# A spectral mixer: a smaller first constant table, its masks, two moved loads and a new order of the jobs

## The chip, the cores and the metric

The kernel runs on one core of one Trainium2 chip. Its time is the device time of one execution in microseconds (us); the number compared is the median of several runs. A core has five engines that work at the same time and meet only at semaphores: TensorE (PE: matmuls, with weight loads shown as PEld), VectorE (DVE), ScalarE (ACT), GpSimd (POOL) and SyncE (SP). SP, ACT and POOL also issue DMAs, each on a queue of its own, in the order of its instructions.

## The reference

Two spectral filters on one input `x` (2048 x 1024), mixed by a gate for each row. Both filters have the same input, so only their products with the weights differ:

```python
X = jnp.fft.rfft2(x.astype(jnp.float32), axes=(-2, -1))
X = X * (w_r + 1j * w_i)                          # weights 2048 x 513
y = jnp.fft.irfft2(X, s=(S, D), axes=(-2, -1)).astype(jnp.bfloat16)
...
g = jax.nn.sigmoid((x * gate_w).sum(-1, keepdims=True))
return g * a + (1 - g) * b                        # a, b: y for the weights A and B
```

## The kernel before, in words

The two-dimensional transforms are built from matmuls with small tables of cosines and sines, in stages:

- **Stage 1** (L463, L457): the first step of the transform over rows. `x` comes in eight chunks c (two loads each, `xload`, L362: one by SP, one by ACT for c < 4, both by SP after). `prep` (L426, job `pp`) lets DVE write a reversed copy of half of a chunk into a zone; chunk 6 is folded by an addition and a subtraction instead. Each chunk gives two jobs `s1.c.j` of eight matmuls: four read `x` itself, four the reversed copy. The right-hand side is the table M of cosines and sines, and M times +1, -1 by partition, made by the jobs `mv.c.k` (`mvariant`, L417, on DVE at L424 or on ACT at L422) with scales from the sign table SM. M holds a column for each of two halves of the partitions (b), zero where a partition belongs to the other half: 2048 columns. It is loaded in four pieces (`MP`, L355; `mload`, L358). ACT or DVE then copies a job's 1024 columns out of PSUM (`evict1`, L467, recorded at the copy helpers L329 and L332).
- **Stage 2** (L494, jobs `s2`) and **stage 4** (L509, `s4`) give the spectrum, in two sets of columns: M (upper) and O (lower), eight units each; ACT empties PSUM after each (`e2`, `e4`). Units 2q and 2q+1 of stage 4 make pair q. Pairs lie in three slots (`direct`, L351), and their exchanged twins in two (`swapped`).
- **Exchange** (`swap`, L519, jobs `sw`): two POOL DMAs swap the odd and even partitions of a pair.
- **Products** (`product`, L529, recorded at L539): DVE multiplies a pair (D) and its exchanged twin (S) by the weights, in two halves: `D.M.0.1` is set M, pair 0, half 1. The upper halves of M's products must be done before the weights of set O (`wo`, L843) may be loaded over M's.
- **Stage 5** (L601, jobs `s5`, 32 of them): the first step back; groups 16 to 31 need all M products, 0 to 15 all O products. ACT (and DVE twice) empties PSUM (`e5`). `edge` (L664) puts right a few special columns.
- **Gate**: `gate_weights`, `gate_spectrum` (L554) and `row_sums` (L573) get the gate's row sums from the spectrum; they go to DRAM (`gate_rows`), come back broadcast to all partitions (`rows_in`, L637, job `zl`, two loads ZB0 and ZB1), and go through a sigmoid on ACT (L645, `sg`), a sign on DVE (L649, `gm`) and 16 products with the table U5 on DVE (L657, `rb`).
- **Stages 6 and 7** (L708, L732): the steps to the output rows; ACT and DVE (L776) finish them, SP stores.

The order of the jobs is written out by hand in `PLAN` (L151): a list of tokens, name, arguments, for jobs on PE the PSUM unit (0 to 3, two banks each), and the engine (`a` ACT, `d` DVE). Each engine runs its jobs in that order; the class `Prog` (L200) turns reads and writes of named buffers into semaphore waits. Before the first job stand 11 matmuls on zeros (L379); `IDLE` (L442) puts a few more matmuls whose result is not used ahead of two jobs of stage 1.

The loads at the start stand in this order. SP: M0, x chunk 0 (second half), M1, x chunks 1, 2, 3 (first halves), M3, then x chunks 4 to 7 and the weights. ACT: x chunk 0 (first half), chunk 1 (second half), M2, chunks 2 and 3 (second halves). POOL: SM. `late_loads` (L617) brings U5 and another table behind the last exchange, on SP, after the gate broadcast.

Of the kernel before, what the change touches and what calls it, by code (L numbers as in the profile page):

```python
# [5 lines left out]
ACT = mybir.ActivationFunctionType  # L6
# [16 lines left out]
def make_consts():  # L23
# [4 lines left out]
    M = np.zeros((128, 32, 16, 2, 2))  # L28
    for b in range(2):
        on = 1.0 * (pb == b)[:, None]  # L30
        n = 64 * n1[:, None] + 32 * b + np.arange(32)[None, :]
        for t in range(16):
            if t == 0:
                M[:, :, 0, 0, b] = on
                M[:, :, 0, 1, b] = on * ((-1.0) ** n1)[:, None]
            else:
                ph = pi2 * t * n / 2048
                M[:, :, t, 0, b] = on * np.cos(ph)
                M[:, :, t, 1, b] = -on * np.sin(ph)
    C["M"] = M.reshape(128, 2048)  # L40
# [58 lines left out]
    blocks += [np.ones((128, 128))]  # L99
# [15 lines left out]
    SM = np.zeros((128, 5), np.float32)  # L115
# [4 lines left out]
    SM[:, 4] = -1.0  # L120
    C["SM"] = SM
# [30 lines left out]
mv.0.3..d mv.0.2..d mv.0.1..d pp.0..d s1.0.0.0.pe mv.1.3..d mv.1.2..a mv.1.1..d s1.0.1.1.pe e1.0.0..a e1.0.1..d  # L152
mv.3.3..a mv.2.2..a mv.3.2..a mv.2.3..d mv.2.1..a pp.1..d s1.1.0.2.pe mv.3.1..a s1.1.1.3.pe e1.1.0..a pp.2..d
s1.2.0.0.pe e1.1.1..a s1.2.1.1.pe pp.3..d e1.2.0..a s1.3.0.2.pe e1.2.1..a mv.4.2..d mv.5.2..d s1.3.1.3.pe
mv.4.1..d e1.3.0..a mv.4.3..d pp.4..d s1.4.1.0.pe mv.6.1..d e1.3.1..a mv.5.1..d mv.7.1..d s1.4.0.1.pe mv.7.3..d
pp.5..d e1.4.1..a mv.7.2..d mv.5.3..d e1.4.0..a s1.5.0.2.pe pp.6..d s1.5.1.3.pe e1.5.0..a s1.6.0.0.pe pp.7.0..d
e1.5.1..a pp.7.1..d s1.7.0.1.pe e1.6.0..d s1.6.1.2.pe e1.7.0.0..a s1.7.1.3.pe e1.7.0.1..d e1.6.1..a
s2a.M.0.0.pe e1.7.1.1..d e1.7.1.0..a s2a.M.1.1.pe s2b.M.0..pe s2.M.2.2.pe e2.M.0..a s2b.M.1..pe e2.M.2..a
s4.M.0.3.pe e2.M.1..d s2.M.3.0.pe e4.M.0..a s4.M.1.2.pe e2.M.3..a s4.M.2.1.pe e4.M.1..a s4.M.3.3.pe e4.M.2..a
D.M.0.1..d sw.M.0..dma gw.0.pe s2.M.5.2.pe e4.M.3..a D.M.0.0..d s2.M.4.1.pe egw..a sw.M.1..dma e2.M.5..a  # L160
gs.1.3.pe e2.M.4..a D.M.1.1..d s4.M.5.0.pe egs.1..a s4.M.4.2.pe D.M.1.0..d e4.M.5..a gs.3.1.pe e4.M.4..a
s2.M.7.3.pe S.M.0.1..d egs.3..a s2.O.1.0.pe e2.M.7..a S.M.0.0..d gs.2.2.pe e2.O.1..a S.M.1.1..d s4.M.7.1.pe
sw.M.2..dma egs.2..a s2.M.6.3.pe S.M.1.0..d e4.M.7..a gs.0.0.pe e2.M.6..a D.M.2.1..d s2.O.0.2.pe egs.0..a
# [103 lines left out]
def bass_gated_mix__spectral_gfnet__spectral_gfnet__prompt_kernel(nc, A_x, A_w_r, A_w_i, B_x, B_w_r, B_w_i, gate_w, out):  # L267
# [25 lines left out]
    VT = sb("VT", 512, f32)  # L293
    SM = sb("SM", 5, f32)
# [23 lines left out]
    ONo = ck(22)  # L318
# [36 lines left out]
    MP = ((0, 4), (4, 8), (8, 16), (16, 32))  # L355
    mpiece = lambda r: next(i for i, (a, b) in enumerate(MP) if a <= r < b)

    def mload(i, eng):  # L358
        a, b = MP[i]
        dma(eng, f"M{i}", sl(XR, 64 * a, [(1, 64 * (b - a))]).bitcast(u16), cst["M"].ap()[:, 64 * a:64 * b], w=[("M", i)])  # L360
# [21 lines left out]
    dma("pool", "SM", SM[:], cst_sm.ap(), w=["SM"])  # L382
# [34 lines left out]
    def mvariant(eng, c, k):  # L417
        o, i = sl(XR, 2048 * k + 256 * c, [(1, 256)]), sl(XR, 256 * c, [(1, 256)])
        kw = dict(r=[("M", mpiece(4 * c)), "SM"], w=[("MV", c, k)])
        sc = SM[:, {1: 2, 2: 4, 3: 3}[k]:][:, :1]  # L420
        if eng == "act":
            P.add("act", lambda e: e.activation(o, i, ACT.Copy, scale=sc), **kw)  # L422
        else:
            P.add("dve", lambda e: e.tensor_scalar(out=o, in0=i, scalar1=-1.0 if k == 2 else sc, scalar2=None, op0=ALU.mult), **kw)  # L424

    def prep(c, j=None):  # L426
# [7 lines left out]
        for h in (1, 0):  # L434
# [514 lines left out]
```

## Time and profile before

| | |
|---|---|
| Time, median of 3 runs | 121.89 us (121.63 to 122.32) |
| The profiled execution's own time | 122.8 us |
| Its span, from the first to the last recorded instruction | 121.0 us |
| TensorE clock granted, mean | 0.997 of full speed |
| DMA traffic | 26.87 MB, 222 GB/s on average |
| M table, four loads | 64, 64, 128 and 256 KB |
| CK table, its last load (CL) | 416 KB |

The page of the profile gives the busy time of each engine, the span in 40 slices, the chain of work that ended last (each step led back to what released it), and groups of equal instructions: engine, operation, output <- input, shape, count, then busy time and mean duration, then the idle time of the engine ahead of them with what ended it. The chain and the timelines have one piece in a line: start and duration in us, engine, buffer, source line, count. A name such as `L601` is line 601 of the kernel. Engine names with a q (SPq, ACTq) are the instruction queues that issue DMAs; the view of DMA issues has, last in a line, the time from issue to landing.

### The profile page before, as it was taken

To read this page: it belongs to the slowest core of one execution; us is meant where nothing else is said; L and a number is where in the kernel's file an instruction comes from. 1 tells how busy PE (TensorE), PEld (TensorE's weight loads), DVE (VectorE), ACT (ScalarE), POOL (GpSimd) and SP (SyncE) were. 2 spreads that over 40 slices of the span, in tenths; PEclk is the share of its full clock that TensorE was granted. 3 is DMA by queue.
4 is the path that set the end of the run, shared out by engine and by line. 5 is a ranking of instruction groups with operands and counts; after the bars stand their busy time and mean duration, and the time that the engine had idled before them with its cause. 6 is when DMAs were issued, how large, how long until landed. Compare 5 with 4: busy or idle time off the path is not lost.

```text
span 121.0 us, 3622 instructions
## 1 busy us (share of the span) xinstructions
PE 113.5 (94%) x1546; PEld 99.1 (82%) x1546; DVE 85.8 (71%) x127; ACT 103.5 (86%) x127; POOL 17.3 (14%) x37
## 2 busy tenths in 40 slices
PE   6979999999999999789999989999899999999990
PEld 2358899969689787488799989999899989999980
DVE  0375667319679969999979917999503879787772
ACT  0498999699878999979999989999979688988861
POOL 4000009306003393030530000000000000000000
PEclk9999999999999999999999999999999999999998
DMA  2999999999999999649893999300000334443344
GB/s 61 296 331 370 348 360 332 321 319 344 371 350 325 353 306 256 185 108 277 152 371 117 297 381 418 122 0 5 0 0 5 126 134 173 176 175 119 146 175 173
DMA packets 27519, 26.87 MB, mean 222 GB/s; under 512 B 10208, under 2 KB 23216, under 8 KB 27248
## 3 DMA queue, kind: packets, MB, share of 16 engines
q1 hardware_dynamic: 24368, 20.85, 55.8%
q0 software_dynamic: 1760, 4.49, 10.2%
q10 hardware_dynamic: 1376, 1.31, 3.5%
q8 instruction: 12, 0.20, 0.7%
q14 instruction: 3, 0.02, 0.1%
HBM read 18.23 MB, written 4.20 MB: 185 GB/s over the span
## 4 chain that ended last, share of the span: by engine, by line
PE 42%; DVE 17%; DMA 16%; ACT 12%; issue 5%; SPq 4%; POOL 0%; DVEq 0%; ACTq 0%; POOLq 0%
PE PS L732 11%; PE PS L708 10%; PE PS L463 10%; DMA XR<-XR 10%; ACT WB L329 9%; DVE WA L539 9%; DVE WB L539 5%; PE PS L601 5%; SPq L326 4%; DMA WA<-in_B_w_i_dram 4%; PE PS L494 3%; DMA SM<-c_SM 3%; ACT XR L329 2%; ACT WA L329 2%; DVE WA L776 1%
## 5 line engine op out<-in xcount | busy, mean ns | idle before, releaser
L601 PE MATMUL PS<-CK,WA 128*128 128x128 bf16 x256 | 31.8, 223 | 1.6 <-DVE WA L539 1.6
L601 PEld LDWEIGHTS PS<-CK,WA 128*128 128x128 bf16 x256 | 31.3, 145 | 1.9 <-DVE WA L539 1.9
L329 ACT ACTIVATE XR<-PS 128x1024 bf16<-128x1024 f32 x31 | 29.5, 1035 | 2.9 <-PE PS L494 1.6
L329 ACT ACTIVATE WB<-PS 128x1024 bf16<-128x1024 f32 (+1 forms) x31 | 30.8, 1040 | 1.4 <-PE PS L601 1.2
L601 PE MATMUL PS<-CK,WB 128*128 128x128 bf16 x256 | 31.9, 226 | 0.0
L601 PEld LDWEIGHTS PS<-CK,WB 128*128 128x128 bf16 x256 | 31.3, 145 | 0.1
L329 ACT ACTIVATE WA<-PS 128x1024 bf16<-128x1024 f32 (+5 forms) x34 | 25.3, 807 | 5.5 <-PE PS L708 2.8
L776 DVE TENSOR_TENSOR WA<-PS,WA 128x512 bf16<-128x512 f32 (+1 forms) x30 | 19.7, 711 | 10.7 <-ACT WA L329 10.5
L539 DVE TENSOR_TENSOR WB<-XR,WA 128x2048 bf16<-128x2048 bf16 x16 | 19.1, 1222 | 3.3 <-ACT XR L329 2.6
L539 DVE TENSOR_TENSOR WA<-XR,WA 128x2048 bf16<-128x2048 bf16 x16 | 18.7, 1224 | 2.9 <-DMA XR<-XR 2.8
L732 PE MATMUL PS<-FT,WA 128*128 128x256 bf16 x140 | 17.6, 273 | 0.2 <-ACT WA L329 0.2
L494 PE MATMUL PS<-F,FT 128*128 128x128 bf16 x256 | 16.0, 219 | 0.0
L494 PEld LDWEIGHTS PS<-F,FT 128*128 128x128 bf16 x256 | 14.8, 98 | 0.9
L509 PE MATMUL PS<-XR,CK 128*128 128x512 bf16 (+1 forms) x72 | 15.3, 355 | 0.0
L732 PEld LDWEIGHTS PS<-FT,WA 128*128 128x128 bf16 x140 | 13.1, 98 | 1.6 <-ACT WA L329 0.4
L708 PE MATMUL PS<-XR,WB 128*128 128x128 bf16 x208 | 13.6, 219 | 0.5 <-ACT WB L329 0.4
L708 PEld LDWEIGHTS PS<-XR,WB 128*128 128x128 bf16 x208 | 12.5, 98 | 1.0 <-ACT WB L329 0.8
L329 ACT ACTIVATE FT<-PS 128x1024 bf16<-128x1024 f32 (+1 forms) x14 | 12.4, 988 | 0.3 <-PE PS L463 0.3
L326 POOL DMA_DIRECT2D XR<-XR x16 | 8.4, 529 | 25.1 <-DVE WA L539 12.5
L509 PEld LDWEIGHTS PS<-XR,CK 128*128 128x128 bf16 x72 | 6.5, 97 | 5.1 <-ACT XR L329 0.2
L463 PE MATMUL PS<-XR,WB 128*128 128x256 bf16 x56 | 8.4, 273 | 0.9 <-DMA WB<-in_A_x_dram 0.6
L463 PE MATMUL PS<-XR 128*128 128x256 bf16 x56 | 8.4, 273 | 0.2 <-DVE XR L332 0.2
(74 smaller groups left out, 88.1 us busy)
## 6 DMA issues: line engine op xcount, KB each, us to landing
XR<-XR POOLq DMA_DIRECT2D x16, 256.0 KB, 4.9
out_dram<-WA SPq DMA_DIRECT2D x15, 256.0 KB, 2.0
WB<-in_A_x_dram SPq DMA_DIRECT2D x12, 256.0 KB, 6.9
FT<-c_U SPq DMA_DIRECT2D x2, 1024.0 KB, 9.6
WA<-in_A_w_r_dram SPq DMA_DIRECT2D x7, 192.5 KB, 4.9
WA<-in_A_w_i_dram SPq DMA_DIRECT2D x7, 192.5 KB, 5.0
WA<-in_B_w_r_dram SPq DMA_DIRECT2D x7, 192.5 KB, 5.0
WA<-in_B_w_i_dram SPq DMA_DIRECT2D x7, 192.5 KB, 5.9
```

The source lines that it names most:

```text
L326: return P.add(eng, lambda e: e.dma_start(dst, src), dma=name, **kw)
L329: return P.add("act", lambda e: e.activation(dst, src, ACT.Copy), **kw)
L463: P.add("pe", lambda e, o=ps(u * 1024 + q * 256, [(1, 256)]), lh=lh, rh=rh, s=s, q=q: e.matmul(o, lh, rh, start=(s == 0 and q % 2 == 0), s ...
L494: P.add("pe", lambda e, o=o, lh=fblock(cmb, j, t), j=j, rh=rh, cmb=cmb: e.matmul(o, lh, rh, start=(j == 0 and cmb == 0), stop=(j == 1), sk ...
L509: P.add("pe", lambda e, o=o, fb=FB[kind, pm, m], m=m, rh=rh: e.matmul(o, sl(CK, fb, [(1, 128)]), rh, start=(m == 0), stop=(m == 1)), r=["C ...
L539: pop[st, q, sw, half] = P.add("dve", lambda e: e.tensor_tensor(out=o, in0=x, in1=w, op=ALU.mult), r=xr(o_, 2048) + wk, a=[("prod", st, sw ...
L601: P.add("pe", lambda e, o=o, lh=sl(t, to + l0, [(hp, 128)]), ab=ab: e.matmul(o, lh, KI(ab), start=(ab == 0), stop=(ab == 1)), r=[("prod", ...
L708: P.add("pe", lambda e, o=o, lh=lh, rh=rh, cp=cp: e.matmul(o, lh, rh, start=(cp == 0), stop=(cp == 1)), r=[("Z", pi), ("RB", r)], w=[("ps" ...
L732: P.add("pe", lambda e, lh=lh, rh=rh, st=st, sp=sp: e.matmul(ps(bank * 512 + o, [(1, 256)]), lh, rh, start=st, stop=sp), r=[("Y", r), "DI" ...
L776: P.add("dve", lambda e, s=s, op=op: e.tensor_tensor(out=sl(WA, outc(r) + 512 * s, [(1, n), (2, 256)]), in0=ps(2 * u * 512, [(256, n), (1, ...
```

## The change

1. **M without zeros.** The table is stored with one column for both halves of the partitions: 1024 columns in three pieces, rows 0 to 4, 4 to 16 and 16 to 32 (32, 96 and 128 KB). It is loaded to a place of its own; two new variants, k = 0 and 4, spread it: M times a mask that is 1 on the one half of the partitions and 0 on the other. SM gets the two masks as columns 5 and 6. The variants 1, 2 and 3 are made from those two, for a whole piece at a time (twice the piece's columns), and a stage 1 job waits for all that it uses before its first matmul.
2. **Order of columns.** The right-hand sides of stage 1 are now 32 columns from each of four places for each half of the transform's sign (eight pieces of 32 in 256, where four pieces of 64 stood); the PSUM output is written in pieces of 32 so that `evict1` reads the halves next to each other, and FT has another layout, from which stage 2 reads blocks of 128 as before.
3. **Loads.** SM is issued first on ACT's queue instead of POOL's. M2 is issued by ACT after chunk 2, not after chunk 1; there is no M3.
4. **Gate broadcast.** Both loads of `rows_in` also wait for the last exchange.
5. **Memory.** A block of ones at the end of CK goes (CL 416 to 384 KB); the tile VT of `row_sums` goes, and its data lie in the region that CL fills later.
6. **Job table.** `PLAN` is a new list: the same jobs of stages 2 to 7, in another order and on other PSUM units; `mv` jobs by piece; `e1.0.1` on ACT and `e1.2.0` on DVE, where it was the other way round; `e4.M.0` on DVE instead of `e2.M.1`; in stage 5, `e5.10` and `e5.15` on DVE instead of `e5.5` and `e5.13`. The matmuls of `IDLE` are 8 and 4 of 128 columns instead of 4 and 2 of 256.

```diff
-    MP = ((0, 4), (4, 8), (8, 16), (16, 32))
+    MP = ((0, 4), (4, 16), (16, 32))
     mpiece = lambda r: next(i for i, (a, b) in enumerate(MP) if a <= r < b)
+    msize = lambda i: (32 * MP[i][0], 32 * (MP[i][1] - MP[i][0]))
...
-    dma("pool", "SM", SM[:], cst_sm.ap(), w=["SM"])
+    dma("act", "SM", SM[:], cst_sm.ap(), w=["SM"])
...
-        if c == 1:
+        if c == 2:
             mload(2, "act")
-        if c == 3:
-            mload(3, "sp")
...
-    def mvariant(eng, c, k):
-        o, i = sl(XR, 2048 * k + 256 * c, [(1, 256)]), sl(XR, 256 * c, [(1, 256)])
-        kw = dict(r=[("M", mpiece(4 * c)), "SM"], w=[("MV", c, k)])
-        sc = SM[:, {1: 2, 2: 4, 3: 3}[k]:][:, :1]
+    def mvariant(eng, i, k):
+        a, n = msize(i)
+        if k in (0, 4):
+            o, src, r = sl(XR, 256 * k + a, [(1, n)]), sl(XR, 12288 + a, [(1, n)]), [("M", i)]
+        else:
+            o, src, r = sl(XR, 2048 * k + a, [(1024, 2), (1, n)]), sl(XR, a, [(1024, 2), (1, n)]), [("MV", i, 0), ("MV", i, 4)]
+        kw = dict(r=r + ["SM"], w=[("MV", i, k)])
+        sc = SM[:, {0: 5, 4: 6, 1: 2, 2: 4, 3: 3}[k]:][:, :1]
...
-    IDLE = {(1, 0): 4, (2, 0): 2}
+    IDLE = {(1, 0): 8, (2, 0): 4}
...
-        mk = [("M", mpiece(4 * c))] + [("MV", c, k) for k in ((1,) if c in FOLDED else (1, 2, 3))]
+        i = mpiece(4 * c)
+        mk = [("MV", i, k) for k in ((0, 4, 1) if c in FOLDED else (0, 4, 1, 2, 3))]
...
-            rh = sl(XR, 64 * r, [(4096 * s, 2), (2048, 2), (1, 64)])
+            rh = sl(XR, 32 * r, [(4096 * s, 2), (1024, 4), (1, 32)])
+            o = ps(u * 1024 + q * 256, [(32, 4), (128, 2), (1, 32)])
...
-        copy(eng, sl(FT, j * 2048 + 4 * c + o, [(4096, 4), (32, 64), (1, n)]), ps(u * 1024 + 256 * o, [(64, 4), (1, 64), (256, n)]),
+        copy(eng, sl(FT, j * 8192 + 4 * c + o, [(64, 128), (32, 2), (1, n)]), ps(u * 1024 + 256 * o, [(1, 128), (128, 2), (256, n)]),
...
-                w=[("F2", "M"), ("F2", "O")] if h else ["DZ"], after=[] if h else free_spectra())
+                w=[("F2", "M"), ("F2", "O")] if h else ["DZ"], after=swaps + ([] if h else free_spectra()))
```

The order of the jobs as far as the text speaks of it. Before, start of stage 1, the first pairs and the last M products:

```
mv.0.3..d mv.0.2..d mv.0.1..d pp.0..d s1.0.0.0.pe mv.1.3..d mv.1.2..a mv.1.1..d s1.0.1.1.pe e1.0.0..a e1.0.1..d
mv.3.3..a mv.2.2..a mv.3.2..a mv.2.3..d mv.2.1..a pp.1..d s1.1.0.2.pe mv.3.1..a s1.1.1.3.pe e1.1.0..a pp.2..d
...
s2a.M.0.0.pe e1.7.1.1..d e1.7.1.0..a s2a.M.1.1.pe s2b.M.0..pe s2.M.2.2.pe e2.M.0..a s2b.M.1..pe e2.M.2..a
s4.M.0.3.pe e2.M.1..d s2.M.3.0.pe e4.M.0..a s4.M.1.2.pe e2.M.3..a s4.M.2.1.pe e4.M.1..a s4.M.3.3.pe e4.M.2..a
D.M.0.1..d sw.M.0..dma gw.0.pe s2.M.5.2.pe e4.M.3..a D.M.0.0..d s2.M.4.1.pe egw..a sw.M.1..dma e2.M.5..a
...
s2.O.3.2.pe e4.O.0..a s2.O.2.1.pe S.M.2.0..d wo.0..spq e2.O.3..a st.3.pe s2.O.5.0.pe D.O.0.0..d est..a
sw.O.0..dma e2.O.2..a s4.O.3.2.pe D.M.3.0..d e2.O.5..a s4.O.2.3.pe e4.O.3..a D.M.3.1..d s2.O.4.1.pe e4.O.2..a
s2.O.6.0.pe S.M.3.0..d e2.O.4..a s4.O.5.2.pe S.M.3.1..d e2.O.6..a s4.O.4.3.pe D.O.1.0..d e4.O.5..a sw.O.1..dma
```

After, the same places:

```
mv.0.4..d mv.0.0..d mv.0.1..d mv.0.3..d mv.0.2..d pp.0..d s1.0.0.0.pe mv.1.0..d mv.1.4..a s1.0.1.1.pe e1.0.0..a
mv.1.2..d mv.1.1..d pp.1..d e1.0.1..a mv.1.3..d s1.1.0.2.pe pp.2..d s1.1.1.3.pe e1.1.0..a mv.2.4..d mv.2.0..d
...
s1.7.1.3.pe e1.7.0.1..d e1.6.1..a s2a.M.1.0.pe e1.7.1.1..d e1.7.1.0..a s2a.M.0.1.pe s2b.M.1..pe s2b.M.0..pe
e2.M.1..a s2.M.3.2.pe e2.M.0..a s4.M.1.3.pe e2.M.3..a s4.M.0.0.pe e4.M.1..a gw.1.pe s2.M.2.2.pe e4.M.0..d
egw..a s4.M.3.3.pe e2.M.2..a D.M.0.1..d sw.M.0..dma gs.1.1.pe e4.M.3..a D.M.0.0..d s4.M.2.0.pe egs.1..a
s2.M.6.2.pe e4.M.2..a s2.M.5.3.pe e2.M.6..a D.M.1.1..d sw.M.1..dma s2.M.4.1.pe e2.M.5..a D.M.1.0..d s4.M.6.0.pe
e2.M.4..a s4.M.5.2.pe e4.M.6..a s4.M.4.3.pe S.M.0.1..d e4.M.5..a s2.M.7.1.pe e4.M.4..a S.M.0.0..d gs.0.0.pe
...
s2.O.3.3.pe e4.O.2..a s4.O.1.1.pe
S.M.2.0..d e2.O.3..a wo.0..spq s2.O.4.0.pe e4.O.1..a D.M.3.0..d s4.O.3.2.pe e2.O.4..a sw.O.0..dma D.M.3.1..d
s2.O.5.3.pe e4.O.3..a S.M.3.0..d s4.O.4.1.pe e2.O.5..a s2.O.6.0.pe S.M.3.1..d e4.O.4..a s4.O.5.2.pe e2.O.6..a
D.O.1.0..d sw.O.1..dma s2.O.7.3.pe wo.1..spq e4.O.5..a D.O.0.0..d s5.19.1.pe e2.O.7..a D.O.2.0..d s5.17.0.pe
```

More of the change, by code (lines that the diff above doesn't have):

```diff
@@ L27, in make_consts @@
     n1, pb, dh = p // 4, (p // 2) % 2, p % 2
[L28 to L40, printed above, removed]
+    M = np.zeros((128, 32, 16, 2))
+    n = 64 * n1[:, None] + 32 * pb[:, None] + np.arange(32)[None, :]
+    M[:, :, 0, 0], M[:, :, 0, 1] = 1.0, ((-1.0) ** n1)[:, None]
+    for t in range(1, 16):
+        ph = pi2 * t * n / 2048
+        M[:, :, t, 0], M[:, :, t, 1] = np.cos(ph), -np.sin(ph)
+    C["M"] = M.reshape(128, 1024)
     row = np.arange(128)
@@ L292, in bass_gated_mix__spectral_gfnet__spectral_gfnet__prompt_kernel @@
     PST = sb("PST", 128)
-    VT = sb("VT", 512, f32)
-    SM = sb("SM", 5, f32)
+    SM = sb("SM", 7, f32)
     SM2 = sb("SM2", 1, f32)
@@ L461, in stage1 @@
             lh = sl(XR, 8192 + 1024 * z + 256 * q + 128 * j, [(1, 128)]) if s else sl(WB, r * 512 + 128 * j, [(1, 128)])
-            rh = sl(XR, 64 * r, [(4096 * s, 2), (2048, 2), (1, 64)])
-            P.add("pe", lambda e, o=ps(u * 1024 + q * 256, [(1, 256)]), lh=lh, rh=rh, s=s, q=q: e.matmul(o, lh, rh, start=(s == 0 and q % 2 == 0), stop=(s == 1), skip_group_check=True),
+            rh = sl(XR, 32 * r, [(4096 * s, 2), (1024, 4), (1, 32)])
+            o = ps(u * 1024 + q * 256, [(32, 4), (128, 2), (1, 32)])
+            P.add("pe", lambda e, o=o, lh=lh, rh=rh, s=s, q=q: e.matmul(o, lh, rh, start=(s == 0 and q % 2 == 0), stop=(s == 1), skip_group_check=True),
                   r=[("x", c)] + mk + ([("zone", z)] if s else []), w=[("ps", 2 * u + q // 2)])
@@ L844, in bass_gated_mix__spectral_gfnet__spectral_gfnet__prompt_kernel @@
             if b:
+                assert "rows" in {t.split(".")[0] for t in PLAN.split()[:PLAN.split().index(token)]}
                 dma("sp", "CL", sl(CK, 1280, [(1, NK - 1280)]).bitcast(u16), cst["CK"].ap()[:, 1280:], w=["CL"])
```

87 lines of the change are left out of this document (38 added, 49 removed).

## The prediction

> **What bounds the kernel now.** I read the page first: its span, the engines, and the two groups of ScalarE (ACT) that matter here.
>
> ```profile
> span 121.0 us, 3622 instructions
> PE 113.5 (94%) x1546; PEld 99.1 (82%) x1546; DVE 85.8 (71%) x127; ACT 103.5 (86%) x127; POOL 17.3 (14%) x37
> ...
> GB/s 61 296 331 370 348 360 332 321 319 344 371 350 325 353 306 256 185 108 277 152 371 117 297 381 418 122 0 5 0 0 5 126 134 173 176 175 119 146 175 173
> ...
> L329 ACT ACTIVATE WB<-PS 128x1024 bf16<-128x1024 f32 (+1 forms) x31 | 30.8, 1040 | 1.4 <-PE PS L601 1.2
> ```
>
> PE is busy 94% of the span, and it only begins its real work after 5 us, so no more than a few us can be won between. ACT at 86% is the second bound: in stage 5 it empties PSUM (WB<-PS) and sat idle only 1.4 us before those 31 evictions, 1.2 of it waiting for PE. Then the waits of PE between 5 and 80 us:
>
> ```profile
> PE PS L601 <- DVE WA L539: 1.6, 2, 1.2
> PE PS L463 <- DMA WB<-in_A_x_dram: 0.6, 1, 0.6
> PE PS L463 <- DVE XR L424: 0.3, 1, 0.3
> PE PS L463 <- DVE XR L332: 0.2, 1, 0.2
> ```
>
> Four causes, 2.7 us. The first line is stage 5 (L601) waiting for a product (L539), twice: 1.2 us for the last M product, 0.4 us for the last O product. The others are stage 1. The chain that ended last gives the places:
>
> ```profile
> 1.21 3.38 DMA SM<-c_SM
> ...
> 5.46 1.92 PE PS L463 x16
> ...
> 20.54 2.80 PE PS L494 x48
> ...
> 27.94 6.07 DMA XR<-XR
> ...
> 49.47 2.30 DVE WA L539 x2
> ...
> 57.34 4.39 DMA WA<-in_B_w_i_dram
> ...
> 67.60 2.37 DVE WA L539 x2
> ...
> 70.01 4.06 PE PS L601 x63
> ...
> 77.51 11.25 ACT WB L329 x11
> ...
> 88.81 2.41 PE PS L708 x40
> ```
>
> At the start the chain is the sign table (SM), landed at 4.59, and the variants. From 20.54 it is PE; then a chain of exchanges and products; then the weights of set O, whose loads the M products release; then the O products; then PE again, with ACT in front of it from 77.51 (11 evictions in 11.25 us, 1.02 each). From 88.81 PE is the bound to the end.
>
> **The change, part by part.**
>
> **Start of stage 1.** SM moves from POOL's queue to the head of ACT's; the table M is half as large (pieces of 32, 96, 128 KB where 64, 64, 128, 256 KB stood).
>
> ```profile
> 0.74 0.34 SPq L326 DMA_DIRECT2D XR<-c_M  x1
> 1.13 0.77 SPq L326 DMA_DIRECT2D WB<-in_A_x_dram  x1
> 2.58 1.94 SPq L326 DMA_DIRECT2D WB<-in_A_x_dram  x3
> 5.29 0.43 DVE L332 COPY XR<-WB 128x1024 bf16<-128x1024 bf16 x1
> 8.37 0.61 PE L463 MATMUL PS<-XR,WB 128*128 128x256 bf16 x4 [0.56 <-DMA WB<-in_A_x_dram]
> 8.74 0.42 DVE L332 COPY XR<-WB 128x1024 bf16<-128x1024 bf16 x1
> 9.21 0.61 PE L463 MATMUL PS<-XR 128*128 128x256 bf16 x4 [0.24 <-DVE XR L332]
> 9.86 11.39 ACT L329 ACTIVATE FT<-PS 128x1024 bf16<-128x1024 f32 x13 [0.32 <-PE PS L463]
> ```
>
> ```profile
> XR<-c_M SPq DMA_DIRECT2D x1, 64.0 KB, 2.0
> ...
> WB<-in_A_x_dram SPq DMA_DIRECT2D x1, 256.0 KB, 4.1
> ...
> XR<-c_M SPq DMA_DIRECT2D x1, 64.0 KB, 4.2
> ...
> WB<-in_A_x_dram SPq DMA_DIRECT2D x1, 256.0 KB, 5.7
> ```
>
> These are the issues of the SP queue and, in the second fence, their times to landing: M0 at 0.74 + 2.0 = 2.74, the second half of x chunk 0 at 1.13 + 4.1 = 5.23, M1 (issued at 1.95, behind that half) at 1.95 + 4.2 = 6.15, chunk 1's SP half at 2.58 + 5.7 = 8.28. SM on ACT's queue, by M0's 2.0, lands about 2.8 instead of 4.59, and five variants of 128 and 256 columns are done by about 4.0. But x chunk 0 landed at 5.23, 0.06 ahead of the copy at 5.29: taking 3.4 us out of the chain wins nearly nothing, at most 5.46 - 5.23 = 0.2. Even that is lost, since PE's next 4 x 0.44 us of chunk 0 end near 7.3 and chunk 1 is not there before about 8. So the start is costed at zero, and **chunk 1's landing decides**.
>
> Bounds for that landing: on the SP queue the bytes ahead of it and with it stay 64 + 256 + 64 + 256 = 32 + 256 + 96 + 256 = 640 KB, which says 8.28 again. M2's 128 KB leave ACT's queue ahead of x; at the third slice's 331 GB/s that is 0.39 us, which says 7.9. And M1's 32 KB more, at the 64 KB in 6.15 - 5.23 = 0.92 us of now, say 8.74. I take 8.1, midway between the first two. The Trainium skill, "DMA: Bandwidth & Descriptors", section "Queues, rings and completion order", states that each DMA engine takes turns between the queues that have work, packet by packet; by it, bytes that leave ACT's queue would not hasten SP's, chunk 1 would land at 8.28, and the gain below would be 0.2 us smaller; no row of this trace tells the two apart.
>
> Now the order on DVE. Before, the first four matmuls of chunk 1 started on x alone (8.37) and the other four after the reversed copy (8.74 to 9.17). In the new table the copy pp.1 stands ahead of variant mv.1.3, and stage 1 waits for all five variants before its first matmul. The copy starts at 8.15, the variant about 0.35 later, and the variant is now wide:
>
> ```profile
> L424 DVE TENSOR_SCALAR XR<-XR,SM 128x256 bf16<-128x256 bf16 x12 | 2.9, 280 | 4.0 <-DMA SM<-c_SM 3.5 <-DMA XR<-c_M 0.4
> L422 ACT ACTIVATE XR<-XR,SM 128x256 bf16<-128x256 bf16 x6 | 2.6, 498 | 0.5 <-DMA XR<-c_M 0.5
> L649 DVE TENSOR_SCALAR FT<-FT,SM 128x1024 bf16<-128x1024 bf16 x2 | 1.0, 480 | 0.0
> ```
>
> 280 ns for 256 columns and 480 for 1024 give 0.41 for its 768. PE starts at 8.15 + 0.35 + 0.41 + 0.05 = 8.96, runs four matmuls, and begins the other four at 9.40, 0.19 later than 9.21. From here ACT's 13 evictions in 11.39 us run without a gap until stage 2 has its input, so ACT carries the delay. ACT gives one full eviction to DVE (13 with two halves among them, so 11.39 / 12 = 0.95 each) and gets mv.2.1, 1024 columns: more than the 0.50 of a 256-column variant and about an eviction of as many columns, 1.04 in the page; the 0.1 between them is added. Stage 2 is thus **0.3 us later** (from 0.1 at a landing of 7.9 to 0.9 at 8.74).
>
> The other instructions of the variants (DVE 8192 column writes instead of 6144, in fewer instructions) lie in DVE's gaps. The matmuls of stage 1 read and write 32-column pieces instead of 64; the pace of L463 does not show this form. Every separately addressed column of L686's strided form costs (390 - 219) / 128 = 1.3 ns over a plain 128-column one:
>
> ```profile
> L686 PE MATMUL PS<-WB,CK 128*128 128x128 bf16 x1 | 0.4, 391 | 0.0
> L708 PE MATMUL PS<-XR,WB 128*128 128x128 bf16 x208 | 13.6, 219 | 0.5 <-ACT WB L329 0.4
> ```
>
> Four more pieces in each of 112 matmuls are then 0 to 0.6 us; I take 0, since L708 already reads 64-column pieces at full pace. The new read order of the stage 1 eviction keeps 1024 elements and pieces of four: zero.
>
> **Stages 2 to 4.** The same instructions in a new order. Two things reach the waits at L601. First, D.O.0.0 leaves the queue ahead of the last M products:
>
> ```profile
> 45.88 3.50 DVE L539 TENSOR_TENSOR WB<-XR,WA 128x2048 bf16<-128x2048 bf16 x3
> ```
>
> These three are D.O.0.0, D.M.3.0, D.M.3.1; without the first, the M products end 1.17 us earlier, about the 1.2 that PE waits. Second, the first exchange (27.94, 6.07 us) gets released by e4.M.0, now on DVE, as soon as PE has done five units of stages 2 and 4: 20.54 + 0.3 + 5 x 0.93 (three took 2.80) + 1.2 = 26.7 against the issue that began 0.5 before 27.94, about 0.7 us earlier, and DVE's next products start at its landing. So S.M.3.1 may end up to 1.9 us earlier, the 0.3 counted in, and PE's 1.2 us wait goes. The loads of set O's weights, released by S.M.3.1, move with it, land earlier than 57.34 + 4.39 = 61.73, and the O products should end 1.2 to 1.9 us before 67.60 + 2.37 = 69.97. PE gets there at 69.6 + 0.3 - 1.2 = 68.7, so the 0.4 wait goes too, with little to spare.
>
> But PE may gain only what ACT follows. ACT waited for PE 1.2 us in this stage and from 77.51 it is the bound. So the two waits of PE, 1.6 us, are worth **1.2 us**.
>
> **The gate broadcast** now waits for the last exchange.
>
> ```profile
> 65.47 0.33 SPq L326 DMA_DIRECT2D FT<-gate_rows  x1
> 66.51 0.32 SPq L326 DMA_DIRECT2D FT<-c_U  x1
> 73.07 1.14 ACT L645 ACTIVATE FT<-FT,SM 128x1024 bf16<-128x1024 f32 x1
> ```
>
> ```profile
> FT<-gate_rows SPq DMA_DIRECT2D x1, 512.0 KB, 3.9
> ```
>
> c_U already waits for that exchange and is issued at 66.51, so the broadcast starts 1 us later. Its first half lands in 3.9 us, at 70.4, and sigmoid reads it at 73.07: 2.7 us of cover, so zero. Behind it on SP stand only U5 and DI, which move by the same issue time or less; DVE's sixteen factors, which read them, are not all needed by 88.81. The exchange is rid of 1 us of overlap: 0 to 0.3, taken as 0. VT inside CK makes the CL load wait for the row sums, which stand far ahead of it in both tables: zero. Stages 6 and 7 keep their order apart from bank numbers: zero.
>
> **Sum.** +0.3 - 1.2 = -0.9 us. The profiled execution took 122.8 us (span 121.0 and 1.8 around it), so 121.9; scaled to the median of the runs, 121.89 x 121.9 / 122.8 = **121.0 us**.
>
> **The rivals.**
> - **More.** Chunk 1 lands at 7.9 or before, and ACT follows PE by the whole 1.6 us: 0.1 - 1.6 = -1.5, and -1.8 with the exchange's 0.3: about 120.2. For it: fewer bytes in all by then. Against it: ACT's 1.02 us an eviction.
> - **Nothing to measure.** Stage 5's waits go, but ACT, which has two sigmoids in a row in the new table (2.3 us), is late somewhere else by most of 1.2: 121.9. For it: ACT is the chain at 77.51.
> - **Slower, by a buffer.** There are three slots for a direct pair. In the new table e4.M.5 and e4.M.4 come after e4.M.6, so e4.M.5 is the first to need the slot of pair 0, which the first exchange still reads. ACT gets there after eleven evictions of 0.95 from about 20.54 + 0.3 + 1.4 = 22.2, and two small ones: near 33; all of e4.M.4, e2.M.7 and what follows stand behind it on ACT, and PE behind the full PSUM. If the exchange lands as now (27.94 + 6.07 = 34.0) or 0.3 later with stage 2, ACT loses about 1.1, the chain of products moves with it, and the 1.2 is not won: +0.3 + 0.8 = +1.1, 123.0. It decides at 33: earlier, nothing is lost. Against it: the exchange is released about 0.7 us earlier, which puts the landing at 33.3, at the edge.
> - **The edit does not do what it says.** SM may land late on ACT's queue behind nothing; no row speaks for it, x chunk 0 covers it to 5.23 less 1 us of variants, and no chance is set apart for it.
>
> **How the numbers follow.** Forecast 0.44; more 0.13; nothing 0.24; slower by a buffer 0.19. About 0.5% (0.6 us) is what a measurement of this kernel can tell from no change. Below 121.3 lie the case "more" and most of the forecast: faster 0.52. Within 0.5%: the rest of the forecast and nearly all of "nothing": 0.28. Slower: 0.20. The range runs from 119.8 (a little under "more") to 122.9 (just short of the buffer's full price), leaving out some 0.2. The forecast's own range is 120.3 to 121.7.
>
> **What would show it.** Right: the variants start before 4 us yet the first matmul stays near 5.3; the first matmul of chunk 1 is one block of eight near 9.0; ACT's evictions of stage 1 end 0.2 to 0.4 later than 21.25; the waits of L601 for L539 shrink from 1.6 to under 0.4; stage 6 begins at 87.6 to 88.2. Wrong: chunk 1 landing outside 7.9 to 8.7; ACT or PE waiting for an exchange between 30 and 36 us; ACT idle in 68 to 88 us for edges or sigmoids; a sigmoid waiting for the broadcast.

## The result and the profile after

The changed kernel took 121.56 us (median of 18 runs, 121.05 to 123.86) against 122.40 us for the kernel before (18 runs, 121.52 to 123.17): ratio 0.9935, interval 0.9907 to 0.9962. In a second measurement, with a fresh set of runs, it was 122.01 against 122.17 us: 0.9974 [0.9945, 1.0004]. By these ratios the gain is 0.8 us and 0.3 us, the second with an interval that reaches 1; 121.0 was forecast. The profiled execution of the changed kernel took 121.07 us. Ratios and intervals leave out disturbed executions and are not quotients of the medians given, and the profiled execution of one experiment (D.O.0.0 put back, 124.78 us) was a disturbed one, so its positions are not compared.

The page of the changed kernel: span, engines and the group of stage 5's evictions (`WB<-PS`, 31 of them; then the idle time ahead of them).

```profile
span 119.3 us, 3628 instructions
PE 114.0 (96%) x1552; PEld 99.5 (83%) x1552; DVE 86.0 (72%) x124; ACT 101.9 (85%) x123; POOL 16.8 (14%) x36
...
L320 ACT ACTIVATE WB<-PS 128x1024 bf16<-128x1024 f32 (+1 forms) x31 | 30.8, 1085 | 0.7 <-PE PS L685 0.3
```

The span is 1.7 us shorter, while PE is busy 0.5 us longer, with six matmuls more (those of `IDLE`, 12 where 6 stood): PE waits less. ACT waits 0.7 us ahead of stage 5's evictions, where it waited 1.4. PE's waits between 5 and 80 us:

```profile
PE PS L506 <- ACT XR L320: 0.3, 1, 0.3
PE PS L460 <- issue: 0.2, 1, 0.2
```

The product waits (1.6 us) are gone. A new one of 0.3 us, for ACT in stage 4, has come. The chain that ended last:

```profile
6.07 1.96 PE PS L460 x16
8.64 1.91 PE PS L460 x16
...
20.43 2.82 PE PS L491 x48
...
30.36 5.83 DMA XR<-XR
...
47.82 2.29 DVE WA L536 x2
...
65.06 3.50 DVE WA L536 x3
68.61 7.91 PE PS L600 x127
...
79.39 8.01 ACT WB L320 x8
87.45 2.41 PE PS L707 x40
```

The chain no longer begins with SM. The last O products end at 68.56 (before 69.97) and PE is on the chain from 68.61, 1.40 us earlier than its 70.01 before. Stage 6 begins at 87.45 where it began at 88.81, 1.36 earlier. These are the chain's own marks; the table below takes the first matmul of each stage from PE's timeline, where the last column is the end of PE's last matmul. Every profiled execution here took 4.76 to 4.81 us more than that last mark, so the marks add up to the time.

| Kernel | stage 4 begins | to stage 5 | stage 5 to 6 | stage 6 to the last matmul |
|---|---|---|---|---|
| before | 23.21 | 27.20 | 37.20 | 30.41 |
| after | 23.11 | 27.62 | 35.54 | 30.03 |
| difference | -0.10 | +0.42 | -1.66 | -0.38 |

Sum -1.72 us. The two profiled executions show more than the runs (0.3 to 0.8), since that of before was 0.4 us above its kernel's median and that of after 0.5 us below.

### The profile page after: what moved, and what is told of

Read it like the earlier page. It is cut to its first block, busy times and chain, and to the rows that moved or that the text cites. A ratio compares the mean times of both kernels' runs of the same rounds, so it can differ in the third digit from the quotient of the medians.

```text
span 119.3 us, 3628 instructions
## 1 busy us (share of the span) xinstructions
PE 114.0 (96%) x1552; PEld 99.5 (83%) x1552; DVE 86.0 (72%) x124; ACT 101.9 (85%) x123; POOL 16.8 (14%) x36
## 2 busy tenths in 40 slices
DMA packets 27487, 26.57 MB, mean 223 GB/s; under 512 B 10432, under 2 KB 23312, under 8 KB 27216
## 4 chain that ended last, share of the span: by engine, by line
PE 54%; DVE 20%; DMA 10%; ACT 9%; issue 4%; POOL 0%; DVEq 0%
PE PS L731 12%; PE PS L707 11%; DVE WA L536 11%; PE PS L460 11%; DMA XR<-XR 10%; ACT WB L320 7%; DVE WB L536 7%; PE PS L600 7%; PE PS L372 4%; PE PS L491 3%; PE PS L506 3%; PE PS L685 1%; ACT XR L320 1%; ACT WA L320 1%; PE PS L453 1%
## 5 line engine op out<-in xcount | busy, mean ns | idle before, releaser
L506 PE MATMUL PS<-XR,CK 128*128 128x512 bf16 (+1 forms) x72 | 15.8, 355 | 0.3 <-ACT XR L320 0.3
```

Source lines behind the costliest of these rows:

```text
L506: P.add("pe", lambda e, o=o, fb=FB[kind, pm, m], m=m, rh=rh: e.matmul(o, sl(CK, fb, [(1, 128)]), rh, start=(m == 0), stop=(m == 1)), r=["C ...
```

## The experiments

The theory: the gain is the two product waits of stage 5, and it comes from the place of D.O.0.0 behind the last M products; the new start gains nothing, or costs. The rivals: the start gains (SM and M land earlier, fewer bytes); the first exchange comes earlier because e4.M.0 is on DVE; the gate's new wait matters. The job tables of these kernels have other line breaks, so their line names shift by a few.

**The start alone.** The changed code and the new table to the end of stage 1, the old table from stage 2.

```diff
...
-e1.7.0.1..d e1.6.1..a s2a.M.1.0.pe e1.7.1.1..d e1.7.1.0..a s2a.M.0.1.pe s2b.M.1..pe s2b.M.0..pe
+e1.7.0.1..d e1.6.1..a s2a.M.0.0.pe e1.7.1.1..d e1.7.1.0..a s2a.M.1.1.pe s2b.M.0..pe s2.M.2.2.pe
...
```

> The changed code and the new job table up to the end of stage 1, then the old table from stage 2 on. Theory of the order (the prediction's): the start is worth about nothing (-0.2 to +0.4 us against the kernel before, ratio 0.998 to 1.003), and the waits of PE at stage 5 for the last M and the last O product come back, together 1.0 to 1.8 us. Rival, theory of the loads: the gain is the smaller table and the earlier chunk 1; ratio about 0.993 with this half alone.

122.7 against 122.32 us: 1.0016 [0.9981, 1.0051]. The start by itself gains nothing. PE's waits from 4 to 80 us:

```profile
PE PS L458 <- DVE XR L417: 1.9, 1, 1.9
PE PS L598 <- DVE WA L534: 1.0, 1, 1.0
PE PS L458 <- DMA WB<-in_A_x_dram: 0.5, 1, 0.5
```

The wait of stage 5 for a product (second line) is there, as before, and one of 1.9 us in stage 1. Its timeline, around the reversed copy of chunk 1 (landed at 2.58 + 6.6 = 9.18):

```profile
9.18 0.43 DVE L321 COPY XR<-WB 128x1024 bf16<-128x1024 bf16 x1 [1.57 <-DMA WB<-in_A_x_dram]
9.52 0.41 DVE L417 TENSOR_SCALAR XR<-XR,SM 128x768 bf16<-128x768 bf16 x1
10.19 0.60 PE L458 MATMUL PS<-XR,WB 128*128 128x256 bf16 x4 [1.85 <-DVE XR L417]
```

The copy waits for the load, the wide variant stands behind the copy, and PE waits for the variant: 1.0 us from the landing to the first matmul. Before, it was 0.1 (8.28 to 8.37).

**The order alone.** The code of before and its stage 1 jobs, the new table from stage 2.

```diff
...
-e1.7.0.1..d e1.6.1..a s2a.M.0.0.pe e1.7.1.1..d e1.7.1.0..a s2a.M.1.1.pe s2b.M.0..pe s2.M.2.2.pe
+e1.7.0.1..d e1.6.1..a s2a.M.1.0.pe e1.7.1.1..d e1.7.1.0..a s2a.M.0.1.pe s2b.M.1..pe s2b.M.0..pe
...
```

> The kernel before, with its own loads, tables and stage 1 jobs, and the new job table from stage 2 on. Theory of the order: about -0.8 to -1.4 us, ratio 0.989 to 0.994, with no wait of stage 5 for the last M product. Theory of the loads: no gain, ratio 0.998 to 1.002, whatever the waits do, because ACT bounds stage 5.

121.8 against 122.32 us: 0.9964 [0.9936, 0.9993], between the two measurements of the whole change (0.9935 and 0.9974). PE's waits:

```profile
PE PS L461 <- DMA WB<-in_A_x_dram: 0.6, 1, 0.6
PE PS L507 <- ACT XR L327: 0.3, 1, 0.3
PE PS L461 <- DVE XR L330: 0.2, 1, 0.2
```

No wait for a product; and the 0.3 us for ACT in stage 4 (L507) has come with the table, not with the start. The rival of the start falls.

**One job in the old table.** The kernel before with D.O.0.0 behind S.M.3.1, nothing else; measured twice.

```diff
...
-st.3.pe s2.O.5.0.pe D.O.0.0..d est..a
+st.3.pe s2.O.5.0.pe est..a
...
-S.M.3.1..d e2.O.6..a s4.O.4.3.pe D.O.1.0..d
+S.M.3.1..d D.O.0.0..d e2.O.6..a s4.O.4.3.pe D.O.1.0..d
...
```

> The kernel before with one job moved: D.O.0.0 stands behind S.M.3.1 on DVE. Theory of the order: the wait of PE for the last M product falls from 1.2 us to under 0.2, the O weights are issued 1.1 us earlier, and the kernel gains 0.5 to 1.1 us (ratio 0.991 to 0.996): this one job is most of the whole change. Rival: the wait moves to the O products or to ACT, ratio 0.998 to 1.002.

> The kernel before with D.O.0.0 behind S.M.3.1, measured beside the changed kernel. Theory (this one job is the gain): within 0.3% of the changed kernel. Rival (the other edits of the table bring half of it): 0.3% or more slower than the changed kernel.

122.07 against 122.32 us, 0.9969 [0.9938, 1.0000], and 121.8 against 122.17 us, 0.9971 [0.9944, 0.9998]: less than the 0.991 to 0.996 that was expected, and the first interval ends at 1. PE's waits between 4 and 80 us in the first of the two:

```profile
PE PS L461 <- DMA WB<-in_A_x_dram: 1.3, 1, 1.3
```

No product is waited for any more; the second has one wait of 0.2 us, before the O groups. DVE's timeline with the last M products, of the first:

```profile
47.75 2.38 DVE L537 TENSOR_TENSOR WA<-XR,WA 128x2048 bf16<-128x2048 bf16 x2
50.03 2.36 DVE L537 TENSOR_TENSOR WB<-XR,WA 128x2048 bf16<-128x2048 bf16 x2
```

The pair S.M.3.0 and S.M.3.1 ends at 50.13 (D.O.0.0 follows), in a kernel whose stage 4 began 0.33 later than that of before, where S.M.3.1 ended at 51.77. In stage 5, moving one job does to the traces what the whole table does: it takes 35.48 and 35.56 us here, 35.54 in the changed kernel, 37.20 before.

**The same job put back in the changed kernel.**

```diff
...
-s2.O.4.0.pe e4.O.1..a D.M.3.0..d s4.O.3.2.pe
+s2.O.4.0.pe e4.O.1..a D.O.0.0..d D.M.3.0..d s4.O.3.2.pe
...
-e4.O.5..a D.O.0.0..d s5.19.1.pe
+e4.O.5..a s5.19.1.pe
...
```

> The changed kernel with one job moved: the product D.O.0.0 stands ahead of D.M.3.0 on DVE again, as in the old table. Theory of the order: the last M product ends 1.1 to 1.2 us later (about 51.2 instead of 50.1), PE waits 0.4 to 0.8 us at the start of stage 5, and the whole is 0.3 to 0.8 us slower than the changed kernel (ratio to before 0.996 to 1.000). Rival: the chain has slack, nothing changes (ratio 0.993).

122.45 against 122.32 us: 1.0024 [0.9995, 1.0052]. Without this place of the one job, the gain is gone: the interval lies above that of the order alone, measured beside it (0.9936 to 0.9993). The waits of L598 for a product are back; in this execution of 124.78 us that shows where PE waits, not how long it does otherwise:

```profile
PE PS L598 <- DVE WA L534: 2.4, 2, 1.5
```

**e4.M.0 on ACT again** (and e2.M.1 on DVE, as before).

```diff
...
-s2b.M.0..pe e2.M.1..a s2.M.3.2.pe
+s2b.M.0..pe e2.M.1..d s2.M.3.2.pe
...
-s2.M.2.2.pe e4.M.0..d egw..a
+s2.M.2.2.pe e4.M.0..a egw..a
...
```

> The changed kernel with the eviction e4.M.0 on ACT and e2.M.1 on DVE. Theory of the prediction: the first exchange is issued 0.5 to 1.0 us later than 26.6, S.M.3.1 ends later by as much, and PE waits 0.1 to 0.7 us at the start of stage 5; ratio to before 0.994 to 0.998. Rival: the exchange chain has slack behind D.O.0.0's move, nothing changes (0.9935).

121.98 against 122.29 us: 0.9981 [0.9952, 1.0010]; not to be told from the changed kernel. The issue of the first exchange by POOL, here and (second fence) in the changed kernel:

```profile
27.09 1.05 POOL L315 DMA_DIRECT2D XR<-XR  x2 [2.83 <-ACT GW L318]
```

```profile
26.57 1.06 POOL L317 DMA_DIRECT2D XR<-XR  x2 [2.62 <-ACT GW L320]
```

That is 27.09 - 23.80 = 3.29 us after the first matmul of stage 4 here, and 26.57 - 23.11 = 3.46 after it in the changed kernel; before it was 27.43 - 23.21 = 4.22. The earlier exchange comes with the new order of PE's units and ACT's evictions, and stays with e4.M.0 on ACT; there is no product wait at stage 5 here either.

**mv.1.3 ahead of the reversed copy**, to undo the serial order on DVE.

```diff
...
-mv.1.2..d mv.1.1..d pp.1..d e1.0.1..a mv.1.3..d s1.1.0.2.pe
+mv.1.2..d mv.1.1..d mv.1.3..d pp.1..d e1.0.1..a s1.1.0.2.pe
...
```

> The changed kernel with one job moved on DVE: the variant mv.1.3 stands ahead of the reversed copy pp.1, so that the first four matmuls of chunk 1 can start when chunk 1 lands, as in the old table. In the profiles so far the changed start code lost 0.2 to 1.9 us of PE there, by when chunk 1 landed. Theory (the serial copy and variant cost): the first matmul of chunk 1 begins 0.1 us after the landing instead of 1.0, stage 1 ends 0.4 to 0.5 us earlier for the same landing, ratio to before about 0.990 (the change itself 0.9935). Rival (ACT or the landing of later chunks bounds stage 1): no difference, 0.9935.

121.64 against 122.29 us: 0.9966 [0.9941, 0.9992]. Its timeline (chunk 1 landed at 8.67):

```profile
8.73 0.43 DVE L321 COPY XR<-WB 128x1024 bf16<-128x1024 bf16 x1 [0.80 <-DMA WB<-in_A_x_dram]
...
8.75 0.61 PE L458 MATMUL PS<-XR,WB 128*128 128x256 bf16 x4 [0.57 <-DMA WB<-in_A_x_dram]
```

PE starts with the copy, 0.08 us after the landing, and from the landing to stage 4 are 14.96 us, where the changed kernel has 15.54. So 0.6 us comes back in the trace. The time was expected near 0.990 and is not measurably another one than the changed kernel's.

**Put together:** the changed code, mv.1.3 first, SM second on ACT's queue, and from stage 2 the old table with D.O.0.0 late.

```diff
-    dma("act", "SM", SM[:], cst_sm.ap(), w=["SM"])
...
     xload(0, 0, "act")
+    dma("act", "SM", SM[:], cst_sm.ap(), w=["SM"])
...
-mv.1.2..d mv.1.1..d pp.1..d e1.0.1..a mv.1.3..d s1.1.0.2.pe
+mv.1.2..d mv.1.1..d mv.1.3..d pp.1..d e1.0.1..a s1.1.0.2.pe
...
-e1.7.0.1..d e1.6.1..a s2a.M.1.0.pe e1.7.1.1..d e1.7.1.0..a s2a.M.0.1.pe s2b.M.1..pe s2b.M.0..pe
+e1.7.0.1..d e1.6.1..a s2a.M.0.0.pe e1.7.1.1..d e1.7.1.0..a s2a.M.1.1.pe s2b.M.0..pe s2.M.2.2.pe
...
-S.M.3.1..d e4.O.4..a s4.O.5.2.pe e2.O.6..a D.O.1.0..d
+S.M.3.1..d D.O.0.0..d e2.O.6..a s4.O.4.3.pe D.O.1.0..d
...
```

> A version that should beat both: the changed loads and tables, mv.1.3 ahead of pp.1, SM second on ACT's queue (behind the first half of x chunk 0), and from stage 2 on the old job table with D.O.0.0 behind S.M.3.1. Theory: stage 5 waits for no product (as where this one job was moved in the kernel before), stages 2 to 4 take 27.2 us as in the old table and not 27.6 as in the new one, the first matmul of stage 1 is 0.3 to 0.6 us earlier than in the changed kernel: ratio to before 0.985 to 0.990. Rival (the whole new table is needed): 0.993 or more.

122.05 against 122.29 us: 0.9997 [0.9971, 1.0024]. It was expected at 0.985 to 0.990; it is no gain at all, though its interval overlaps those of its parts. Of its DMA issues, that of SM:

```profile
SM<-c_SM ACTq DMA_DIRECT2D x1, 3.5 KB, 3.5
```

SM needs 3.5 us behind x chunk 0 on ACT's queue, where it needs 1.9 at its head; the first matmul is at 6.29 instead of 5.6 to 5.9, and stage 4 begins at 24.20. But the late SM is not what PE waits for later on. PE's waits in stage 1 after the first matmul, with chunk 1 landed at 8.87:

```profile
9.00 0.60 PE L458 MATMUL PS<-XR,WB 128*128 128x256 bf16 x4 [0.36 <-DMA WB<-in_A_x_dram]
...
12.54 0.60 PE L458 MATMUL PS<-XR,WB 128*128 128x256 bf16 x4 [0.53 <-issue]
```

Chunk 1 covers chunk 0 here too: the first block of chunk 1 begins 0.13 us after its landing. The second wait has no cause in this view; DVE starts the reversed copy of chunk 3 in the same moment (12.54), after a wait for a load, and chunk 3's second half landed at 4.14 + 8.3 = 12.44. From chunk 1's landing to stage 4 are 15.33 us, 0.37 more than with mv.1.3 first alone. Stages 2 to 4 take 27.2 us as with any old table, and stage 5 takes 35.63: in the trace the job's move does what it did alone, and part of what the start won goes to the wait at 12.54. Why the median gains nothing stays open.

**SM on POOL's queue again.**

```diff
-    dma("act", "SM", SM[:], cst_sm.ap(), w=["SM"])
+    dma("pool", "SM", SM[:], cst_sm.ap(), w=["SM"])
```

> The changed kernel with SM on POOL's queue again. SM lands at 4.6 instead of 2.65, five variants are done at about 5.7; the first half of x chunk 0 leads ACT's queue again and lands about 1 us earlier than 5.8. Theory of the prediction: zero in the time; the first matmul at 5.6 to 5.9 as in the changed kernel, since variants and chunk 0 change places as the last to come. Rival (the sign table's place is part of the gain): 0.3% or more slower than the changed kernel.

121.51 against 122.17 us: 0.9955 [0.9933, 0.9976]; the changed kernel measured beside it has 0.9974 [0.9945, 1.0004]. The first variants:

```profile
4.72 0.93 DVE L419 TENSOR_SCALAR XR<-XR,SM 128x128 bf16<-128x128 bf16 x4 [3.58 <-DMA SM<-c_SM]
```

They start 2 us later than in the changed kernel (2.73), and the first matmul comes at 5.94, as late as in the others. SM's new place is worth nothing, and it may cost: the two intervals overlap, but 9 of the 12 runs of the changed kernel beside it took longer than the longest of these 12 (121.79). No other experiment tests that.

**The gate broadcast without its new wait**, measured twice.

```diff
-                w=[("F2", "M"), ("F2", "O")] if h else ["DZ"], after=swaps + ([] if h else free_spectra()))
+                w=[("F2", "M"), ("F2", "O")] if h else ["DZ"], after=[] if h else free_spectra())
```

> The changed kernel with the gate broadcast no longer waiting for the last exchange. Theory of the prediction: zero; at most 0.3 us, because the broadcast overlaps the last exchange by a us or not at all (ratio 0.9935, from 0.991 to 0.996). Rival (the broadcast disturbs the last exchange, which the last O products wait for): the last product ends 0.5 us or more later and PE waits for it, ratio 0.997 or more.

> The changed kernel without the broadcast's wait for the last exchange, beside the changed kernel. Its profile showed no wait for a product in stage 5, so the theory of zero expects it within 0.3% of the changed kernel here; the rival (the wait is worth 0.5%, as the ratio of the first measurement would have it) expects it 0.4% or more slower.

121.93 against 122.29 us, 0.9993 [0.9965, 1.0021], and 122.0 against 122.17 us, 0.9998 [0.9974, 1.0022]. In its trace the wait that the instruction queue of SP has ahead of the broadcast, and the broadcast itself:

```profile
SPq L251 <- DMA gate_rows<-AT: 8.0, 1, 8.0
```

```profile
62.04 0.56 POOL L317 DMA_DIRECT2D gate_rows<-AT  x1
...
65.18 0.33 SPq L317 DMA_DIRECT2D FT<-gate_rows  x1
```

And in the changed kernel, the last exchange, the write of the gate's row sums, the broadcast and the sigmoid:

```profile
60.88 1.04 POOL L317 DMA_DIRECT2D XR<-XR  x2 [1.23 <-ACT WB L320]
61.91 0.56 POOL L317 DMA_DIRECT2D gate_rows<-AT  x1
...
64.38 0.33 SPq L317 DMA_DIRECT2D FT<-gate_rows  x1
...
74.57 1.14 ACT L644 ACTIVATE FT<-FT,SM 128x1024 bf16<-128x1024 f32 x1
```

In the new table the write of the gate's rows stands behind the last exchange on POOL (before, it stood ahead of it: 60.03 and 60.58). The broadcast needs that write, so its own new wait for the exchange is over when it gets there, and taking it away moves nothing: issued at 65.18 and 65.50 without it, 64.38 and 65.54 with it. Yet both ratios without it are near 1, a little above those with it (0.9935 and 0.9974). The medians beside each other, 122.00 without it and 122.01 with it, do not differ, and no row of the traces has a reason for the first ratio; it stays open.

**The changed kernel again**, beside three of these kernels.

```diff
(no edit)
```

> The changed kernel itself, beside the three others on one chip. Expected from its first measurement: ratio to before 0.991 to 0.996. In the profiles so far chunk 1 landed between 7.6 and 9.2 us with the same code, yet stage 5 began at 50.7 to 51.2 wherever stage 4 began between 23.1 and 23.7; if the exchanges set that time, this profile shows the same: stage 5 at 50.7 to 51.2, S.M.3.1 ended at 50.1 to 50.8.

122.01 against 122.17 us: 0.9974 [0.9945, 1.0004]. This execution shows the late case of the start: chunk 1 landed at 8.78 instead of 7.57.

```profile
PE PS L460 <- DVE XR L419: 1.9, 1, 1.9
...
PE PS L600 <- DVE WA L536: 0.2, 1, 0.2
```

PE waits 1.9 us for mv.1.3; stage 4 begins at 24.26, not at 23.11, and all behind it moves with it: 27.62, 35.59 and 30.03 us for the three stretches of the table above, the same to 0.05 us. So the expectation that the exchanges hold stage 5 at 50.7 to 51.2 failed: it began at 24.26 + 27.62 = 51.88. The 1.2 us between the two profiles of one kernel is the landing of one load.

By the intervals against the kernel before, no version was faster than the changed kernel; SM on POOL (0.9955), mv.1.3 first (0.9966) and the one job in the old table (0.9969 and 0.9971) overlap with its 0.9935 and 0.9974. Taken together, the eleven measurements of kernels with D.O.0.0 behind the last M products lie between 0.9935 and 0.9998, and the two with the changed start and D.O.0.0 ahead of them at 1.0016 and 1.0024.

## Why the prediction was right, and where it was not

The time (121.56, forecast 121.0), the sign and the main mechanism came out; three sizes did not.

**The start, costed at zero: right in sum, wrong in its marks.** The changed kernel's timeline and DMA issues:

```profile
0.75 0.36 ACTq L317 DMA_DIRECT2D SM<-c_SM  x1
1.14 2.34 ACTq L317 DMA_DIRECT2D WB<-in_A_x_dram  x3
2.73 0.94 DVE L419 TENSOR_SCALAR XR<-XR,SM 128x128 bf16<-128x128 bf16 x4 [1.59 <-DMA SM<-c_SM]
5.87 0.85 PE L460 MATMUL PS<-XR,WB 128*128 128x256 bf16 x4
7.63 0.43 DVE L323 COPY XR<-WB 128x1024 bf16<-128x1024 bf16 x1
7.97 0.41 DVE L419 TENSOR_SCALAR XR<-XR,SM 128x768 bf16<-128x768 bf16 x1
8.64 0.60 PE L460 MATMUL PS<-XR,WB 128*128 128x256 bf16 x4 [0.17 <-issue]
```

```profile
WB<-in_A_x_dram SPq DMA_DIRECT2D x1, 256.0 KB, 5.0
...
SM<-c_SM ACTq DMA_DIRECT2D x1, 3.5 KB, 1.9
...
WB<-in_A_x_dram ACTq DMA_DIRECT2D x1, 256.0 KB, 4.7
```

SM landed at 0.75 + 1.9 = 2.65 and the variants were done before 4, as said. But the first matmul did not stay near 5.3: it came at 5.87. Behind SM the first half of x chunk 0 was issued at 1.14 and landed at 1.14 + 4.7 = 5.84; before, at 0.75 + 3.6 = 4.35. The step that failed counted what SM's move takes off the chain and not what is queued behind SM. With SM at the head of ACT's queue the first matmul came at 5.57 to 5.94 (seven profiles, mean 5.78), with the code of before at 5.25 to 5.86 (four, mean 5.60), so it is about 0.2 us and no more than the spread. In the traces it cost nothing, since chunk 1 covers it: the time from chunk 1's landing to stage 4 (below) doesn't follow it.

**Chunk 1 decides: right. Its landing at 8.1: not a number that one profile can give.** It landed between 7.57 and 9.18 us in nine profiles with the changed tables (SM on another place in two of them) and between 8.28 and 8.8 in four with the old ones; the means are 8.5 and 8.6. The changed kernel's 7.57 lies outside the 7.9 to 8.7 beyond which the prediction was to be wrong. So M2's later place hastened nothing that can be seen. The prediction quoted from the Trainium skill ("DMA: Bandwidth & Descriptors", section "Queues, rings and completion order") that each DMA engine takes turns between the queues packet by packet, and concluded that bytes that leave ACT's queue would not hasten SP's. The means agree with that; the spread of 1.6 us is too large to prove it, and it is wider than all bounds of this step.

**Stage 2 later by 0.3: right in kind, too small.** One block of eight matmuls after copy and variant, at 8.64 where 9.0 was said. From the landing to stage 4 are 15.45 to 15.73 us in seven profiles with the serial order, and 14.76 to 14.93 in three of four with the old start (15.51 in the fourth, where an eviction on DVE ended late and held up the copy); with mv.1.3 first it is 14.96. The means, 15.52 and 14.87 of the three, differ by 0.7 us (by 0.5 with the fourth), and 15.52 and 14.96 by 0.6, where the term was 0.3 for a landing of 8.1. ACT's evictions of stage 1 still ended at 21.14, not 0.2 to 0.4 later than 21.25, as chunk 1 landed early in that execution.

**Pieces of 32 columns, taken as 0 of 0 to 0.6: right.** Stage 1's matmuls of the reversed copy, before and after:

```profile
L463 PE MATMUL PS<-XR 128*128 128x256 bf16 x56 | 8.4, 273 | 0.2 <-DVE XR L332 0.2
```

```profile
L460 PE MATMUL PS<-XR 128*128 128x256 bf16 x56 | 8.4, 273 | 0.0
```

One of 256 columns takes 273 ns in both.

**The product waits: right in place and cause.** D.O.0.0 alone takes them away in the old table, and brings them back in the new one. Two parts of the step failed. First, "e4.M.0, now on DVE" does not release the exchange earlier; the new order of units does, with e4.M.0 on either engine, and in the old table the waits go without it. Second, "the two waits of PE, 1.6 us, are worth 1.2", because ACT bounds stage 5: in the profiles it was all won, 1.66 us. From the chain's O groups to stage 6 the kernels take 88.81 - 70.01 = 18.80 and 87.45 - 68.61 = 18.84 us: ACT paces that stretch, but it starts when PE does, so it moves with it and takes nothing back; stage 6 began at 87.45, just ahead of the 87.6 to 88.2 that was forecast. By the ratios the single job is worth only 0.38 and 0.35 us. The profiled execution of before took 0.4 us more than its median, and the start alone, which has the early D.O.0.0 too, shows 1.04 us of such waits and 36.39 us from stage 5 to 6, so 0.8 to 0.9 more than the 35.5 without them, not 1.7; how much of them a median execution has wasn't traced.

**Stages 2 to 4 and 6 to 7, costed at zero: two small terms of opposite sign.** From stage 4 to stage 5 the old table takes 27.2 us in all five profiles that have it there; the new one 27.6 to 27.7 in six of eight, five of them with a wait of 0.3 us for ACT near 37 us, and 27.2 in the other two. From stage 6 to the last matmul the old table takes 30.41 in all five, the new one 30.02 to 30.03 in all eight: 0.38 less, of which 0.18 in the kernel before is a PE idle time ahead of 98.89, where the old chain goes through DVE and ACT. The prediction read the tables wrongly there ("Stages 6 and 7 keep their order apart from bank numbers"): rows 0 and 1 change places in the new one (s6a.0 ahead of s6a.1, and s7, `cq` and `ad` with them), and DVE's last three gate jobs (rb.13, rb.11, dn) stand behind the first jobs of stage 6. No experiment tells which of these does it.

**The gate, zero: right in size, for another reason** than the 2.7 us of cover: the row sums' write goes behind the last exchange itself, and the broadcast was issued at 64.38, earlier than before (65.47). The two ratios near 1 without the wait stay unexplained.

**The rivals.** The wait for a buffer is real, but rare and small. Of the profiles with the new order one has it, the second of the gate broadcast without its wait; ACT waits there for an exchange:

```profile
34.98 2.85 ACT L320 ACTIVATE XR<-PS 128x1024 bf16<-128x1024 f32 x3 [0.47 <-DMA XR<-XR]
```

That is where the rival put it, with 0.5 us instead of 1.1, and stages 2 to 4 are hardly longer by it (27.69 us). The changed kernel's own two profiles do not have it. "Nothing to measure" is close to the second measurement, though not by ACT being late in stage 5.

The sum by the traces: start +0.6, stages 2 to 4 +0.4, stage 5 -0.4 (by the single job's ratios) to -1.7 (by the two profiles), tail -0.4, so +0.2 to -1.1 us. The ratios of the whole change, -0.3 and -0.8 us, lie within. That the forecast's -0.9 lies so near the first of them is in part luck: the start was priced too low, stages 2 to 4 and the tail at nothing, stage 5 by a bound that in fact moves along with the start of its stretch, and these errors have opposite signs. How much of stage 5's 1.7 us a median execution gains is the size that stays open.

## What to carry to other kernels

When an engine's queue holds work for a later stage ahead of the last work of the present one, moving that one job is worth trying before a new table: here it measured 0.9969 and 0.9971 by itself, beside 0.9935 and 0.9974 for the whole change. A bound that paces a later stretch moves along when the stretch starts earlier, so it doesn't eat a gain made before it. One profile shows where a wait is, not how long the median execution waits: compare waits over several profiles before pricing them.

## What the hardware showed that was not expected

- The landing of one 256 KB load at the start differs by up to 1.6 us between executions of the same loads (7.57 to 9.18 us), and PE's marks behind it move by as much (stage 4 at 23.11 and 24.63).
- With a load of 3.5 KB at the head of ACT's queue, the 256 KB behind it landed 1.5 us later in the profiled execution (4.35 before, 5.84 after, issued 0.39 us later); in all, it landed at 5.3 to 5.9 us in seven profiles with that load ahead of it and at 3.9 to 4.5 in six without. Behind that load, the 3.5 KB take 3.5 us instead of 1.9.
- With the same instructions on PE from stage 6 on, two orders of them differ by 0.38 us, each the same to 0.01 us in its profiles (five and eight).
- Right-hand sides and PSUM outputs in pieces of 32 columns, where 64 stood, left a stage 1 matmul of 256 columns at 273 ns.
